# A fused attention and gated-MLP kernel: exponentials behind both shares, wider attention operations, and a band block one slot sooner

## Chip, cores and metric

The kernel runs on one core of a Trainium2 chip. The metric is the device time of one execution in microseconds (us). Every ratio below is the mean time of one kernel's fast runs over the mean of the other's fast runs of the same rounds, so it is not quite the ratio of the medians that stand beside it. A difference counts as faster or slower only beyond 2%.

## The reference

Two branches on the same kind of input, mixed by a gate. Branch A is attention in which each position sees 8 earlier ones, two apart. Branch B is a gated MLP whose second half is normalized and mixed along the sequence.

```python
x = A_x                                             # 1 x 2048 x 1024
g = sigmoid((x * gate_w).sum(-1, keepdims=True))
# A: 32 heads of 32, window W = 8, dilation 2
q, k, v = split(x @ wqkv)
logits = einsum('bhsd,bhswd->bhsw', q, gathered(k)) * scale   # masked where idx < 0
a = einsum('bhsw,bhswd->bhsd', softmax(logits), gathered(v)) @ wo
# B: F = 3584, Fh = F // 2
z = gelu(B_x @ w_in);  z1 = z[..., :Fh];  z2 = layernorm(z[..., Fh:])
b = ((z1 * (w_sp @ z2 + b_sp)) @ w_out)
return g * a + (1 - g) * b
```

## The kernel before

The kernel is one long stream of products on the matrix engine (PE). Most are Strassen-like sets ("quads") of 7 products with 4 PSUM banks. The attention is done by the vector engine (DVE) beside them, in 8 groups of heads; a Python scheduler decides at build time, by an estimated clock, which piece of attention work is put next on DVE and where loads and exponentials go. The first part makes q, k, v and the band products; then come the "z2 pairs", pairs of quads for the second half of branch B. The parts that matter here, with their lines:

```python
# band_blocks(g, first, step, n): q-k products of one group, into banks 4..7
st = band_slots[band_at[0] % 3]; band_at[0] += 1
...
nc.tensor.matmul(banks[4 + h][...], qt[...], kt_[...], ...)     # L355
...
nc.scalar.copy(dst, src)                                         # L363: empties all four banks
# ... then stores of st to band_d, issued by SP (the sync engine)

# strassen(...): one quad                                        (cut)
last_seed[0] = nc.scalar.copy(Y[:, n], X[:, n])                  # L421: seed copy
share(vs, V[:, n])                                               # L427: share copy, into vq_slots
nc.scalar.copy(Z[:, n], Y[:, n])                                 # L432
# chain(...): one lean quad                                      (cut)
last_add[0] = nc.vector.tensor_tensor(out, a, vs, ALU.add)       # L474: the plus
last_seed[0] = nc.scalar.copy(Y[:, n], X[:, n])                  # L487
share(vs, V[:, n])                                               # L493

def mark(bs, N=512, lo=0):                                       # L559: two products that open a new stretch
    for b in bs: nc.tensor.matmul(b[:, lo:N], ...)

def exponential(g): nc.scalar.activation(L[:], L[:], ACT.Exp, ...)   # L631

# maxima(): first operation on a group's logits, waits for their load
tt(att_m[:], L4[:, :, 0:4, :], L4[:, :, 4:8, :], ALU.max)        # L640, then L641 to L643
# products(): attention weights times v, and the sum over the window
for ws in SPLIT[g > FINE]:
    ... tt(p5[:, ws], in0[:, ws], in1[:, ws], ALU.mult)          # L677, 128x2048
for n, ws in enumerate([slice(0, 4)] if g <= FINE else [slice(0, 2), slice(2, 4)]):
    ... tt(a, a, b, ALU.add)                                     # L681, 128x2048

BAND_AT = (1, 3, 6)
def among_bands(g, quad):                                        # groups 2 and 4
    for n in range(7):
        next(quad); step()
        if n + 1 in BAND_AT: band_set(g, x); ...

def quad_step():                                                 # in each z2 pair
    hold[0] = count[0] != 1        # exponentials may go out at this step only
    ...
```

A seed copy starts one bank with the sum that stands in another; PE then goes on adding into it. A share copy takes a sum out of PSUM; in the lean quads a plus on DVE then adds it to what stands in a bank. The last of the three band slots overlaps the memory that the share copy L427 writes into, so the first L427 after the bands of group 2 waits until the store of a band block has left it.

## Time and profile before

| | before |
|---|---|
| time, median of 3 runs | 650.38 us (650.0 to 650.91) |
| span of the profiled run | 649.2 us |
| PE busy | 638.1 us, 98% |
| DVE busy, ACT busy | 519.3 us, 297.8 us |
| waits of PE that the change can reach | 4, of 0.15 to 0.35 us (85.17, 88.03, 189.56, 192.89 us) |

PE's records say when a matmul starts. A wait shows as a gap, and what ended it stands in brackets. Since PE carries everything, I read the result below by the time between two products that all versions share, instead of by the total, in which the start-up alone scatters by over 1 us:

- S1, from the gate product (L996, 44.50 us before, behind all start-up) to the first band products of group 3 (116.15): it holds the band blocks of group 2. Before: 71.65 us.
- S2, from the mark that opens the first z2 pair (183.45; called T below) to the last mark but one (264.06). Before: 80.61 us.

### The profile page before, as it was taken

Reading aid. Unit: us, or ns where it says so; the run is one execution under the profiler, and the core shown is the slowest. Engines: PE = TensorE matmul, PEld = TensorE weight load, DVE = VectorE, ACT = ScalarE, POOL = GpSimd, SP = SyncE. Lnnn points to the kernel's source line nnn. Section 1 sums busy time; section 2 is a strip of 40 time slices with the busy share of each in tenths; the row PEclk is TensorE's granted clock in tenths of the full one; section 3 lists DMA queues with packets and bytes.
Section 4 is the critical chain, followed back from the end, with each engine's and each line's share of the span. In section 5 each row is a group of like instructions: output and inputs, shape, how many; then the busy total and the mean of one; then the engine's idle time right before and its main releaser. Section 6 shows DMA issues by size and latency. Waiting matters only on the chain.

```text
span 649.2 us, 11298 instructions
## 1 busy us (share of the span) xinstructions
PE 638.1 (98%) x4346; PEld 336.4 (52%) x4391; DVE 519.3 (80%) x816; ACT 297.8 (46%) x644; POOL 15.4 (2%) x27
## 2 busy tenths in 40 slices
PE   8999999999999999999999999999999999999997
PEld 4544467444445555444444444444444444868684
DVE  0357988999899999999988766987569999596952
ACT  3547677676776877799643121121121121212110
POOL 2210000000000000001000000000000000000000
PEclk9999999999999999999999999999999999999999
DMA  9979564798688012258994578469587383665401
GB/s 207 198 179 269 126 152 103 175 230 200 122 214 204 1 42 85 66 148 230 258 269 133 130 163 172 120 195 280 100 189 172 86 157 99 111 138 128 124 27 49
DMA packets 227174, 98.19 MB, mean 151 GB/s; under 512 B 174496, under 2 KB 214064, under 8 KB 227120
## 3 DMA queue, kind: packets, MB, share of 16 engines
q1 hardware_dynamic: 226256, 95.70, 61.2%
q0 software_dynamic: 576, 1.57, 0.9%
q8 instruction: 34, 0.56, 0.3%
q10 hardware_dynamic: 288, 0.20, 0.1%
q14 instruction: 20, 0.16, 0.1%
HBM read 44.31 MB, written 36.61 MB: 125 GB/s over the span
## 4 chain that ended last, share of the span: by engine, by line
PE 84%; ACT 4%; DVE 4%; DMA 4%; SPq 2%; issue 2%; ACTq 0%; DVEq 0%
PE psum_all L403 69%; PE psum_all L1487 8%; PE psum_all L293 4%; PE psum_all L303 2%; DMA band_d<-arena 2%; ACT arena L839 2%; PE psum_all L355 1%; DVE arena L677 1%; ACT arena L1178 1%; SPq L189 1%; DVE arena L681 1%; SPq L178 1%; DMA arena<-in_A_wqkv_dram 1%; SPq L194 1%; DVE psum_all L474 1%
## 5 line engine op out<-in xcount | busy, mean ns | idle before, releaser
L403 PE MATMUL psum_all<-arena 128*128 128x512 f16 (+6 forms) x2482 | 503.0, 362 | 3.4 <-issue 0.6
L403 PEld LDWEIGHTS <-arena 128*128 128x128 f16 (+1 forms) x2518 | 245.1, 98 | 253.8 <-issue 4.0
L677 DVE TENSOR_TENSOR arena<-arena,att_A 128x2048 f16<-128x2048 bf16 x64 | 75.5, 1219 | 0.3
L474 DVE TENSOR_TENSOR psum_all<-psum_all,arena 128x512 f32<-128x512 f32 (+1 forms) x78 | 51.0, 669 | 10.1 <-PE psum_all L403 8.3
L1487 PE MATMUL psum_all<-arena 128*128 128x256 f16 (+1 forms) x468 | 51.6, 273 | 0.0
L1487 PEld LDWEIGHTS <-arena 128*128 128x128 f16 x468 | 45.8, 98 | 5.5
L293 PE MATMUL psum_all<-arena 128*128 128x512 bf16 x183 | 42.0, 379 | 1.4 <-issue 0.8
L421 ACT COPY psum_all<-psum_all 128x512 f32<-128x512 f32 (+1 forms) x24 | 12.5, 521 | 66.8 <-PE psum_all L403 66.2
L784 ACT ACTIVATE arena<-psum_all 128x448 bf16<-128x448 f32 x64 | 34.3, 546 | 19.0 <-PE psum_all L403 9.0
L1178 ACT ACTIVATE arena<-psum_all 128x512 bf16<-128x512 f32 x56 | 31.4, 612 | 19.8 <-PE psum_all L403 9.0
L681 DVE TENSOR_TENSOR arena<-arena 128x2048 f16<-128x2048 f16 x32 | 37.9, 1218 | 0.0
L363 ACT CAST arena<-psum_all 128x1988 f16<-128x1988 f32 (+3 forms) x25 | 34.0, 1360 | 3.6 <-PE psum_all L355 3.4
L839 ACT ACTIVATE arena<-arena 128x896 bf16<-128x896 bf16 x32 | 30.9, 980 | 0.0
L546 DVE TENSOR_TENSOR arena<-arena 128x512 f16<-128x512 bf16 (+5 forms) x60 | 30.1, 534 | 0.3
L445 ACT COPY psum_all<-psum_all 128x512 f32<-128x512 f32 (+1 forms) x24 | 12.4, 519 | 37.2 <-PE psum_all L403 36.6
L293 PEld LDWEIGHTS <-arena 128*128 128x128 bf16 x192 | 18.1, 98 | 21.6 <-DMA arena<-in_A_wqkv_dram 0.7
L870 ACT CAST arena<-psum_all 128x512 bf16<-128x512 f32 x40 | 22.1, 592 | 12.5 <-DVE psum_all L474 9.6
L389 DVE TENSOR_TENSOR arena<-arena 128x2048 f16<-128x2048 bf16 x8 | 9.4, 1222 | 21.8 <-ACT gl_s L306 20.9
L427 ACT COPY arena<-psum_all 128x512 f32<-128x512 f32 (+1 forms) x24 | 12.7, 534 | 26.3 <-PE psum_all L403 22.5
L487 ACT COPY psum_all<-psum_all 128x512 f32<-128x512 f32 (+1 forms) x39 | 21.7, 570 | 6.6 <-PE psum_all L403 6.0
L432 ACT COPY psum_all<-psum_all 128x512 f32<-128x512 f32 (+1 forms) x24 | 12.5, 519 | 25.6 <-PE psum_all L403 23.0
L550 DVE TENSOR_TENSOR arena<-arena 128x1024 f16<-128x1024 f16 (+1 forms) x16 | 11.3, 714 | 15.7 <-PE psum_all L403 15.7
(113 smaller groups left out, 530.6 us busy)
## 6 DMA issues: line engine op xcount, KB each, us to landing
arena<-v_d SPq DMA_DIRECT2D x8, 960.0 KB, 7.1
z_d<-arena SPq DMA_DIRECT2D x14, 512.0 KB, 3.4
arena<-z_d SPq DMA_DIRECT2D x14, 512.0 KB, 4.1
zg_d<-arena SPq DMA_DIRECT2D x56, 128.0 KB, 2.2
arena<-zg_d SPq DMA_DIRECT2D x32, 224.0 KB, 3.2
band_d<-arena SPq DMA_DIRECT2D x28, 248.5 KB, 4.6
arena<-in_A_wqkv_dram SPq DMA_DIRECT2D x16, 256.0 KB, 4.3
o_d<-arena SPq DMA_DIRECT2D x4, 1024.0 KB, 6.3
```

The costliest lines, as they stand in the source:

```text
L293: nc.tensor.matmul(ps[:], w[:, t, kt, :], xT[:, kt, 512 * c:512 * (c + 1)], start=(kt == 0), stop=(kt == KT - 1))
L363: nc.scalar.copy(dst, src)
L403: nc.tensor.matmul(bank[:, 0:N], lhsT, rhs, start=(start and m == 0), stop=(m == n - 1), skip_group_check=True)
L474: last_add[0] = nc.vector.tensor_tensor(out[:, n], a[:, n], vs, ALU.add)
L546: return [lambda a=a: nc.vector.tensor_tensor(*a) for a in args]
L677: lambda ws=ws, in0=in0, in1=in1: tt(p5[:, ws], in0[:, ws], in1[:, ws], ALU.mult)), False
L681: lambda a=p3[:, ws], b=p3[:, ws.start + 4:ws.stop + 4]: tt(a, a, b, ALU.add)), not n
L784: nc.scalar.activation(z2[:, i + 8 * a, ZC * c:ZC * (c + 1)], bank[:, 0:ZC], ACT.Gelu_apprx_tanh, accum_out=s1[:, 4 * n + c:4 * n + c + 1])
L839: return nc.scalar.activation(junk, src, ACT.Square, accum_out=(s2, s2h)[x][:, n:n + 1])
L870: nc.scalar.copy((qT_slots, kT_slots)[t][g % 2][:, :, 256 * (c + 2 * x):256 * (c + 2 * x + 1)], bank[:].rearrange("p (n e) -> p e n", e=2))
L1178: last_gelu[0] = nc.scalar.activation(z1s[:, f, a, :], bank[:], ACT.Gelu_apprx_tanh)
L1487: nc.tensor.matmul(bank[:, h], l, r, start=(start and m == 0), stop=(m == len(ab) - 1), skip_group_check=True)
```

## The change

Its intent: release the last exponentials of the attention only when both share copies of a z2 pair are out, so that the pluses of the pair need not wait for ACT; use operations of twice the width where no plus can be held up by them; and put the last band block of group 2 where its evacuation is over by the time the mark needs the banks. In full:

```diff
-                for ws in SPLIT[g > FINE]:
+                for ws in SPLIT[not wide[0]]:
...
-                for n, ws in enumerate([slice(0, 4)] if g <= FINE else [slice(0, 2), slice(2, 4)]):
+                for n, ws in enumerate([slice(0, 4)] if wide[0] else [slice(0, 2), slice(2, 4)]):
...
+    wide = [False]
     SPLIT, FINE = [[slice(n * x, n * x + n) for x in range(8 // n)] for n in (4, 2)], FINE_TO
...
-            if n + 1 in BAND_AT:
+            if n + 1 in (BAND_AT if g != 2 else (1, 3, 5)):
...
         hold[0] = g == NG - 1
+        wide[0] = g in (5, 6, 7)
...
+    wide[0] = False
     load_later(1, clock["PE"] + 3.0, 2.0)
...
-            hold[0] = count[0] != 1
+            hold[0] = count[0] != 4
```

## The prediction

> **What bounds the kernel now.** I read the page's busy table first, then the waits of the matrix engine (PE), then the timelines around those waits, then the chain of waits.
>
> ```profile
> span 649.2 us, 11298 instructions
> PE 638.1 (98%) x4346; PEld 336.4 (52%) x4391; DVE 519.3 (80%) x816; ACT 297.8 (46%) x644; POOL 15.4 (2%) x27
> ```
>
> PE is busy 638.1 of 649.2 us at full granted clock, and the change leaves every matmul in place. Removing work from the Vector engine (DVE, 519.3 us) or the Scalar engine (ACT, 297.8 us) therefore saves nothing by itself: only time in which PE stands still can come back. Of the 11.1 us in which PE is idle, some 2.5 us lie before the kernel is under way (gaps before 12 us) and 3.5 us after the last matmul (645.67 us), and neither is touched. The list of what PE waited for names the rest (us in total, times, longest):
>
> ```profile
> PE psum_all L355 <- ACT arena L363: 0.6, 1, 0.6
> PE psum_all L559 <- ACT arena L363: 0.3, 1, 0.3
> PE psum_all L403 <- ACT psum_all L487: 0.3, 1, 0.3
> PE psum_all L403 <- DVE psum_all L474: 0.3, 1, 0.3
> PE psum_all L403 <- ACT psum_all L421: 0.3, 1, 0.3
> ```
>
> Five waits, 0.3 to 0.6 us each. The timeline of PE puts them at 85.17 (L559), 88.03 (L421), 178.77 (L355), 189.56 (L474) and 259.94 us (L487). Two shorter ones, 0.15 us before 192.89 and 0.12 us before 292.09, show only in finer windows. The "0.16 issue" gaps after band blocks are not waits: 11 matmuls are recorded where the code has 12, so a record is missing there.
>
> Two places belong to the change. The first is group 2:
>
> ```profile
> 79.66 2.54 PE L403 MATMUL psum_all<-arena 128*128 128x512 bf16 x11 [0.16 <-issue]
> 82.12 0.65 PE L355 MATMUL psum_all<-arena 32*64 32x71 bf16 x56
> 82.70 2.12 PE L403 MATMUL psum_all<-arena 128*128 128x512 f16 x12
> 85.17 0.43 PE L559 MATMUL psum_all<-arena 128*128 128x320 bf16 x2 [0.35 <-ACT arena L363]
> 85.44 2.34 PE L403 MATMUL psum_all<-arena 128*128 128x320 bf16 x16
> 88.03 1.25 PE L403 MATMUL psum_all<-arena 128*128 128x320 f16 x8 [0.25 <-ACT psum_all L421]
> ...
> 79.61 1.82 ACT L363 CAST arena<-psum_all 128x1988 f16<-128x1988 f32 x1 [0.74 <-PE psum_all L355]
> 81.32 0.63 ACT L631 ACTIVATE att_L<-att_L 128x512 f16<-128x512 f16 x1
> 81.85 1.55 ACT L870 CAST arena<-psum_all 128x512 bf16<-128x512 f32 x3
> 83.28 1.85 ACT L363 CAST arena<-psum_all 128x1988 f16<-128x1988 f32 x1
> ...
> 87.23 0.43 ACT L427 COPY arena<-psum_all 128x320 f32<-128x320 f32 x1 [1.29 <-DMA band_d<-arena]
> 87.55 0.43 ACT L421 COPY psum_all<-psum_all 128x320 f32<-128x320 f32 x1
> ```
>
> The bands (L355) fill four PSUM banks; ACT empties them in one copy of 1.82 us (L363); the marking matmul L559 needs two of those banks. At 88.03 us PE waits for a seed copy (L421) that stands behind a share copy (L427), and that copy waits for a transfer of bands to leave the memory it writes into.
>
> The second is the first z2 pair:
>
> ```profile
> 184.01 4.62 DVE L677 TENSOR_TENSOR arena<-arena,att_A 128x2048 f16<-128x2048 bf16 x4
> 188.67 0.29 DVE L661 TENSOR_TENSOR att_A<-att_L,att_r 128x256 f16<-128x256 f16 x1
> 188.88 1.16 DVE L474 TENSOR_TENSOR psum_all<-psum_all,arena 128x448 f32<-128x448 f32 x2
> 189.94 2.35 DVE L681 TENSOR_TENSOR arena<-arena 128x2048 f16<-128x2048 f16 x2
> 192.21 1.16 DVE L474 TENSOR_TENSOR psum_all<-psum_all,arena 128x448 f32<-128x448 f32 x2
> ...
> 187.21 0.95 ACT L493 COPY arena<-psum_all 128x448 f32<-128x448 f32 x2
> ```
>
> PE waits for DVE's L474. Its inputs, the share copies (L493), are ready at 187.21 + 0.95 = 188.16 us, before L474 begins at 188.88. DVE came to L474 late, straight out of attention work: here DVE sets the time and ACT doesn't.
>
> **What the Trainium skill says.** "VectorE: DVE Perf Modes", section "The TRN2 errata": operations from SBUF pay a fixed latency each, so a large tile pays it once and small ones each time. The trace agrees: four 2048-wide operations take 4.62 us, so (4.62 - 1.22) / 3 = 1.133 us from start to start, while a 4096-wide one (L1147 starts at 434.48, the next at 436.68) takes 2.20. A merge saves 2 x 1.133 - 2.20 = 0.07 us. "ScalarE: Activation LUTs", section "What ACT_TABLE_LOAD costs", gives 1283 ns for a load and 1380 ns of drain after it. The load is 1283 ns here too, but the drain doesn't show: the load of 185.38 us is followed by its exponential at 186.67. "DMA: Bandwidth & Descriptors", section "Why a DMA increments its semaphore by 16 and not by 1": the engines of a transfer finish independently and all are counted. Here, of the store that L427 waits for, 15 of 16 landings are in by 86.15 us and the last comes at 87.13, after a 16 KB packet of the instruction queue had occupied an engine from 84.46 for 0.96 us.
>
> **The change, part by part.** Matmuls recorded 0.30 or 0.35 us long follow each other faster: 16 of 320 columns in 2.34 us give (2.34 - 0.30) / 15 = 0.136 us from start to start; 512 columns give (2.54 - 0.38) / 10 = 0.216. I count in these steps.
>
> *Bands of group 2 a slot sooner.* Four matmuls of 512 columns (0.86 us) now come after the third band block instead of before it. The bands would start at 82.12 - 4 x 0.216 = 81.26, but the evacuation before them holds the banks until 79.61 + 1.82 = 81.43, and PE wakes some 0.04 us later: 81.47, a new wait of 0.21 us. From there 0.58 us to the next matmul (82.12 to 82.70), 8 x 0.216 and 8 x 0.136: PE reaches the marking matmul at 84.86. ACT's order now has two L870 copies instead of three ahead of the evacuation, which starts near 82.8 and ends near 84.65. So L559 starts at 84.86 instead of 85.17, with no wait: 0.31 us won. But the matmul of 88.03 us, reached at 87.61 before and at 87.30 then, waits for L427, and L427 for the store of the *second* band block, whose evacuation (79.61 to 81.43) hasn't moved. If that store lands at 87.13 again, PE resumes at 88.03 again and the 0.31 us are lost. The store's end hung on an instruction fetch, which follows PE's progress; with the third block 0.65 us earlier it may meet the store at another moment. Landing at 86.15 would remove the wait and yield up to 0.73 us (88.03 to 87.30). I put this part at 0.15 us.
>
> *Wide operations.* The order of the built program has nine merges: six of L677 and three of L681. Worth 9 x 0.07 = 0.6 us of DVE, most of it lost: DVE stands 2.9 us at 169.40 us waiting for a band load, so savings before it vanish. Behind it lie four merges (one L677, one L681, the two that replace the four of 184.01): 0.28 us. L474 moves from 188.88 to 188.60, PE's start from 189.56 to 189.28. PE is ready at 189.12 (the last step before it began at 188.94, plus 0.189 for 448 columns), so a wait of about 0.15 us stays. The wait at 192.89 sits behind the same DVE sequence (L681 twice, unmerged) and moves along: 0.28 us in all, 0.25 with a little doubt.
>
> *Exponentials behind the shares.* In the first pair 1.28 + 0.63 us leave the place ahead of L493, which ends near 186.8 instead of 188.16. L474 wasn't waiting for it: zero. The first gelus shift from 189.47 to about 190.0, into the 2.24 us that ACT then idles before 192.87. The last exponential moves from the fourth pair to the third; its two table loads and 0.63 us fit between the shares (208.8) and the gelus that end at 216.4. Zero for PE.
>
> Sum: 0.15 + 0.25 + 0 = 0.40 us; 650.38 - 0.40 = about 650.0 us. The waits at 178.77, 259.94 and 292.09 us remain.
>
> **Rivals.** (1) *A DMA gate takes the gain of the bands*: the wait at 85.17 goes and the one at 88.03 grows by as much. The unmoved second evacuation speaks for it, the chance position of the fetch against it. Then 650.1. (2) *The share copies were the bound of the first pair*, as the change's description suggests: then both waits there vanish, 0.43 + 0.15 us, and with the bands' 0.31 the time is 649.4. The 0.7 us between the end of L493 and the start of L474 speak against it. (3) *Coarser DVE pieces delay PE*: a 2.2 us operation could stand before an L474 that is needed at once. Against it: wide pieces run only where plain tiles do, which need no L474; the last two end before L474 as the four did. If it happened, +0.3 us. (4) *The exponential of the third pair pushes gelus into PE's bank waits*: up to +1.3 us, one table load; the slack above says no.
>
> **Range and chances.** All that the change can reach on PE is the 0.51 (85.17 - 84.66), 0.41, 0.43 and 0.3 us at four waits, 1.7 us or 0.26%, far below 2%. Runs of the kernel before spread from 650.0 to 650.91. Predicted 650.0; 8 in 10 within 649.1 to 650.9. Faster by over 2%: 0.01; within 2%: 0.98; slower: 0.01.
>
> **What would show it.** A wait of L355 for L363 of about 0.2 us near 81.5; none at L559; the wait for L421 still there at 88 us, with L427 still waiting for the band store; L474 of the first pair about 0.3 us earlier, still straight behind L661, with a smaller wait of PE there; L493 done long before. I am wrong if L427 no longer waits for DMA (more gain), if PE waits at a place with none before, or if the waits after 200 us change size.

## The result, and the profile after

The changed kernel takes 650.11 us in the median (649.78 to 651.18, 6 runs), the kernel before 650.45 us in the same rounds (650.0 to 651.83, 6 runs). The ratio is 0.9995 with a 95% interval of 0.9982 to 1.0008: the same within 2%, and not told from no change at all.

The page of the changed kernel, its span and its busy table:

```profile
span 649.4 us, 11332 instructions
PE 641.5 (99%) x4391; PEld 336.5 (52%) x4391; DVE 518.5 (80%) x807; ACT 297.9 (46%) x644; POOL 15.4 (2%) x27
```

DVE has the nine instructions less (816 to 807) that nine merges make, and is 0.8 us less busy. PE's rise from 638.1 to 641.5 us comes with 45 more recorded matmuls, which were missing from the records before; it is no extra work. The profiled span is 0.2 us *longer* than before, although the median is shorter. The whole list of what PE waited for tells why:

```profile
PE psum_all L303 <- DMA arena<-in_A_x_dram: 1.5, 2, 1.3
PE psum_all L318 <- DVE arena L313: 1.2, 1, 1.2
PE psum_all L355 <- ACT arena L363: 0.6, 1, 0.6
PE psum_all L303 <- DVE arena L325: 0.3, 1, 0.3
PE psum_all L403 <- ACT psum_all L487: 0.3, 1, 0.3
```

In this one execution the first load of the input came 1.3 us late, at 20.5 us, before anything that was changed. All waits that the prediction named as reachable (L559, L474, L421) have left the list. Two gaps too short for this list are new: 0.15 us before the third L355 of group 2 (82.83 us) and 0.14 us at 87.35 us. The waits after 200 us keep their size (0.28 and 0.12 us before, 0.27 and 0.10 us after). By stretches, against the profile before: +1.35 us until the gate product, -0.40 us in S1, -0.76 us in S2, +0.04 us in the rest, +0.22 us at the last product (all from the start times of the same products in both traces).

S1, timeline of the changed kernel around the moved band block, PE and then ACT (columns: start us, us, engine, line, operation, out<-in, count, and in brackets the idle time before and what ended it). Subtract 1.35 to compare with before:

```profile
82.83 0.64 PE L355 MATMUL psum_all<-arena 32*64 32x71 bf16 x56
83.41 2.99 PE L403 MATMUL psum_all<-arena 128*128 128x512 bf16 x16
86.23 0.43 PE L559 MATMUL psum_all<-arena 128*128 128x320 bf16 x2
...
84.15 1.84 ACT L363 CAST arena<-psum_all 128x1988 f16<-128x1988 f32 x1
85.86 1.11 ACT L871 CAST arena<-psum_all 128x512 bf16<-128x512 f32 x2
86.81 0.49 ACT L421 COPY psum_all<-psum_all 128x320 f32<-128x320 f32 x1
88.16 0.42 ACT L427 COPY arena<-psum_all 128x320 f32<-128x320 f32 x1 [0.87 <-PE psum_all L403]
```

The mark L559 starts without a wait, at 86.23 - 1.35 = 84.88 us, 0.29 us sooner than before. But the seed copy L421 starts at 86.81 - 1.35 = 85.46 us, and before it started at 85.46 us as well. ACT simply had one copy L870 (L871 in the changed file, whose later lines stand one lower) ahead of the evacuation moved behind it: between the first evacuation and the seed it does the same work in another order, without a pause. So PE, early at the mark, stands still for the seed: the product at 87.35 us on this trace's own clock starts 0.43 us behind the one before it, where the step is 0.14 us, and the 0.29 us are gone. What S1 did gain comes next: L427 starts at 88.16 - 1.35 = 86.81 us, against 87.23 before, because the band store that it waits for landed sooner. (The bracket names PE, but the product that L427 reads was over by 87.3 us. The store's last landing is recorded at 88.06 us, just ahead of the copy.) The second seed behind L427 is then in time and the 0.41-us step of before vanishes.

S2, timeline of DVE in the changed kernel, and the last share copy of ACT:

```profile
169.56 0.29 DVE L640 TENSOR_TENSOR att_m<-att_L 128x256 f16<-128x256 f16 x1 [2.23 <-DMA att_L<-band_d]
...
184.03 4.49 DVE L677 TENSOR_TENSOR arena<-arena,att_A 128x4096 f16<-128x4096 bf16 x2
188.56 0.29 DVE L661 TENSOR_TENSOR att_A<-att_L,att_r 128x256 f16<-128x256 f16 x1
188.76 1.16 DVE L474 TENSOR_TENSOR psum_all<-psum_all,arena 128x448 f32<-128x448 f32 x2
...
187.25 0.53 ACT L493 COPY arena<-psum_all 128x448 f32<-128x448 f32 x1 [0.23 <-PE psum_all L403]
```

The same wait before the change, from DVE's timeline:

```profile
169.40 0.29 DVE L640 TENSOR_TENSOR att_m<-att_L 128x256 f16<-128x256 f16 x1 [2.88 <-DMA att_L<-band_d]
```

The reader should measure both from the mark T of their own trace (183.45 before, 184.40 after). L640 starts at T - 14.05 before and T - 14.84 after; the plus L474 at T + 5.42 before and T + 4.36 after. So of 1.06 us, 0.79 came because the load of the bands landed sooner relative to PE, and 0.27 from a shorter path on DVE between the two (19.47 to 19.20 us). Which of the two belongs to the change is what the experiments ask.

**Theory A**: the change earns what the two profiles show, 0.40 + 0.76 us. **Theory B**: it earns 0.27 us through the wide operations when the load is late, and something in S1 through the landing of one store; the rest of S2 is when the load that ends the wait at 169 us happens to arrive. **Theory C**, from the change's own description: the exponentials in front of the shares held the pair up.

### The profile page after: what moved, and what is told of

It is laid out like the page before. It is cut to its first block, busy times and chain, and to the rows that moved or that the text cites. A ratio compares the mean times of both kernels' runs of the same rounds, so it can differ in the third digit from the quotient of the medians.

```text
span 649.4 us, 11332 instructions
## 1 busy us (share of the span) xinstructions
PE 641.5 (99%) x4391; PEld 336.5 (52%) x4391; DVE 518.5 (80%) x807; ACT 297.9 (46%) x644; POOL 15.4 (2%) x27
## 4 chain that ended last, share of the span: by engine, by line
PE 90%; ACT 4%; SPq 2%; DMA 1%; DVE 1%; issue 1%; DVEq 0%; ACTq 0%
PE psum_all L403 72%; PE psum_all L1490 8%; PE psum_all L293 6%; PE psum_all L303 2%; PE psum_all L355 2%; ACT arena L840 1%; SPq L178 1%; DMA arena<-in_A_x_dram 1%; ACT arena L1181 1%; PE psum_all L792 1%; ACT arena L785 1%; ACT arena L363 1%; SPq L162 0%; DVE psum_all L474 0%; ACT psum_all L487 0%
## 5 line engine op out<-in xcount | busy, mean ns | idle before, releaser
L677 DVE TENSOR_TENSOR arena<-arena,att_A 128x2048 f16<-128x2048 bf16 (+1 forms) x58 | 74.9, 1329 | 0.3
L474 DVE TENSOR_TENSOR psum_all<-psum_all,arena 128x512 f32<-128x512 f32 (+1 forms) x78 | 51.1, 670 | 11.3 <-PE psum_all L403 8.5
L293 PE MATMUL psum_all<-arena 128*128 128x512 bf16 x192 | 43.3, 379 | 0.1
L421 ACT COPY psum_all<-psum_all 128x512 f32<-128x512 f32 (+1 forms) x24 | 12.5, 521 | 66.1 <-PE psum_all L403 65.4
L681 DVE TENSOR_TENSOR arena<-arena 128x2048 f16<-128x2048 f16 (+1 forms) x29 | 37.7, 1329 | 0.0
L363 ACT CAST arena<-psum_all 128x1988 f16<-128x1988 f32 (+3 forms) x25 | 34.0, 1359 | 3.2 <-PE psum_all L355 2.9
L871 ACT CAST arena<-psum_all 128x512 bf16<-128x512 f32 x40 | 22.1, 593 | 12.5 <-DVE psum_all L474 9.6
L427 ACT COPY arena<-psum_all 128x512 f32<-128x512 f32 (+1 forms) x24 | 12.7, 533 | 26.5 <-PE psum_all L403 23.4
L303 PE MATMUL psum_all<-arena 128*128 128x385 bf16 x128 | 22.7, 330 | 1.8 <-DMA arena<-in_A_x_dram 1.5
```

Of the source, the lines that this page charges most:

```text
L293: nc.tensor.matmul(ps[:], w[:, t, kt, :], xT[:, kt, 512 * c:512 * (c + 1)], start=(kt == 0), stop=(kt == KT - 1))
L303: nc.tensor.matmul(ps[:, 0:VP + 1], xT[:, kt, i * P:(i + 1) * P], wvp[:, kt, :], start=(kt == 0), stop=(kt == KT - 1))
L474: last_add[0] = nc.vector.tensor_tensor(out[:, n], a[:, n], vs, ALU.add)
L677: lambda ws=ws, in0=in0, in1=in1: tt(p5[:, ws], in0[:, ws], in1[:, ws], ALU.mult)), False
L681: lambda a=p3[:, ws], b=p3[:, ws.start + 4:ws.stop + 4]: tt(a, a, b, ALU.add)), not n
```

## The experiments

Twelve runs followed, two of them (e1, e5) of unedited kernels, all correct, all "same" against the kernel before of their own rounds. Their times scatter more than the differences at stake (the kernel before took 650.3 to 655.1 us on the chips of the first two calls), so the findings rest on the stretches, one trace for each run. The expectations name their theories by letters of their own, which each of them explains; only the text between them uses A, B and C as above. This table has the readings of all traces. The times of the S1 group count from the gate product, those of the S2 group from the mark T; all are start times in the trace, in us.

| run | instruction packet: start, length | seed L421 | share L427 released | S1 | L640 | L640 to plus | plus L474 | S2 |
|---|---|---|---|---|---|---|---|---|
| before | 39.97, 0.96 | 40.96 | 42.65 | 71.65 | -14.05 | 19.47 | 5.42 | 80.61 |
| after | 38.20, 1.41 | 40.96 | 42.24 | 71.25 | -14.84 | 19.20 | 4.36 | 79.85 |
| e1 before again | 39.93, 0.93 | 40.96 | 42.62 | 71.62 | -12.92 | 19.47 | 6.55 | 81.72 |
| e2 bands only | 38.07, 1.60 | 40.96 | 42.30 | 71.30 | -12.96 | 19.46 | 6.50 | 81.68 |
| e3 wide only | 39.97, 0.93 | 40.97 | 42.67 | 71.67 | -13.61 | 19.20 | 5.59 | 80.76 |
| e4 exponentials only | 39.95, 0.93 | 40.96 | 42.65 | 71.65 | -14.39 | 19.46 | 5.07 | 80.25 |
| e5 after again | 38.16, 1.56 | 40.96 | 42.34 | 71.35 | -12.98 | 19.19 | 6.21 | 81.38 |
| e6 no share wait | 39.95, 0.93 | 40.96 | 41.32 | 71.24 | -14.31 | 19.47 | 5.16 | 80.34 |
| e7 bands and wide | 38.21, 1.68 | 40.96 | 42.58 | 71.59 | -14.41 | 19.19 | 4.78 | 79.95 |
| e9 load wait filled | 38.19, 1.33 | 40.97 | 42.11 | 71.25 | -11.81 | 16.80 | 4.99 | 80.17 |
| e10 bands, no share wait | 38.06, 1.63 | 40.97 | 41.32 | 71.25 | -14.16 | 19.21 | 5.05 | 80.23 |
| e11 best | 39.94, 0.93 | 40.96 | 41.32 | 71.25 | -13.66 | 17.33 | 3.67 | 79.86 |
| e12 best again | 38.06, 1.52 | 40.97 | 41.32 | 71.25 | -14.63 | 18.31 | 3.68 | 79.86 |

(e8 has another order of PE and is told apart below. "Instruction packet" is the one 16 KB packet of an instruction queue in this stretch.)

Two rules hold over the whole table to 0.02 us:

- S1 = 71.25 + what the release of L427 exceeds 42.24.
- S2 = 79.855 + what the start of the plus exceeds T + 4.68.

They are read from these traces and belong to these orders of work. e8 falls outside both: its S1 is 71.40 with the share released at 42.26, because PE lost 0.14 us at the mark of the group before and the seed came at 41.11; and with another order on DVE its plus starts at T + 5.01 with S2 at 79.96.

The column L640 can be followed one step further back, on the timeline of SP, which gives its instructions in the same order in every run of the table. The second of the two loads that L640 needs is issued at T - 16.88 before, - 17.31 after, - 15.94 in e1, - 15.51 in e5 and - 14.31 in e9, and in all thirteen traces L640 starts 2.5 to 3.0 us behind that. So most of the scatter of 3.0 us is there before the load is issued: SP issues it late. Why was not tried; SP's wait list names the landings of band stores.

### e1: the kernel before, once more

```diff
 (no edit)
```

> The kernel before, unchanged, to learn which of its waits repeat. Two stretches are measured on the matrix engine, free of the start-up: S1 from the gate's matmul to the first bands of group 3 (71.65 us in the first trace of before, 71.25 in that of the changed kernel) and S2 from the marking matmuls of the first z2 pair to those at the head of the z1 stage (80.61 and 79.85). Theory A (the waits follow from the order of the instructions): S1 71.65 and S2 80.61 again within 0.05. Theory B (they follow from when transfers and instruction fetches happen to meet): S1 or S2 moves by 0.2 us or more with no change of the kernel. Total time 650.0 to 651.9 either way.

Measured 651.74 us (650.05 to 653.39), the kernel before 652.31 us in the same rounds, ratio 0.9982 [0.9960, 1.0004]. S1 is 71.62, as in the first trace. S2 is 81.72, 1.11 us more, with nothing changed. DVE's timeline in this run:

```profile
170.29 0.29 DVE L640 TENSOR_TENSOR att_m<-att_L 128x256 f16<-128x256 f16 x1 [3.34 <-DMA att_L<-band_d]
...
189.75 1.16 DVE L474 TENSOR_TENSOR psum_all<-psum_all,arena 128x448 f32<-128x448 f32 x2
```

And the list of PE's waits from 183 to 195 us of the same run (us in total, times, longest):

```profile
PE psum_all L403 <- DVE psum_all L474: 1.4, 1, 1.4
```

The load of the bands let L640 start at T - 12.92, and 19.47 us later, to the hundredth, comes the plus. PE's wait is 1.4 us instead of 0.3. So the 0.76 us that the pair of profiles showed in S2 lie inside the scatter of one and the same kernel. This is against theory A.

### e2: the bands alone

```diff
-            if n + 1 in BAND_AT:
+            if n + 1 in (BAND_AT if g != 2 else (1, 3, 5)):
```

> Only the third band block of group 2 a slot sooner. Theory A1 (order alone): the wait at the marking matmul goes, the wait for the seed copy goes too, S1 falls by 0.4 as in the changed kernel, S2 stays at 80.61. Theory A2 (what is won at the marking matmul is lost one product later to the first seed copy, which now stands behind two output copies): L421 waits of 0.3 us one product after the mark, S1 falls only if the band store lands sooner, by 0 to 0.4. Theory B: S1 anywhere between 71.2 and 71.7. Total time within 0.4 us of before.

Measured 651.13 us (650.63 to 652.4), ratio 0.9978 [0.9958, 0.9997]. S1 is 71.30, 0.35 us under the kernel before; S2 is 81.68 with the late load of this run. The gain in S1 follows the edit.

### e3: the wide operations alone

```diff
-                for ws in SPLIT[g > FINE]:
+                for ws in SPLIT[not wide[0]]:
 ... and the lines that set wide[0]
```

> Only the wide attention operations. Theory A (the Vector engine sets the first z2 pair): S1 stays 71.65, the first L474 of the pair comes 0.28 us sooner, S2 falls by about 0.3. Rival (the share copies behind the exponential are the bound): S2 stays at 80.61, since the exponential still stands ahead of the share copies. Theory B: S2 moves with the wait of L640 for the band load near 169 us. Total time 0 to 0.4 us below before.

Measured 651.36 us (651.03 to 654.69), ratio 0.9988 [0.9962, 1.0014]. S1 unchanged at 71.67. From L640 to the plus DVE takes 19.20 us instead of 19.47, as in the changed kernel. Four merges lie between, so one is worth 0.27 / 4 = 0.067 us. The fall of S2 by 0.3 us, which theory A of this expectation has, did not come: S2 is 0.15 us longer than in the first profile of before, because the load came 0.44 us later.

### e4: the exponentials alone

```diff
-            hold[0] = count[0] != 1
+            hold[0] = count[0] != 4
```

> Only the exponentials moved behind both share copies. Theory A: L493 ends near 187 instead of 188.2, L474 doesn't move, S1 71.65 and S2 80.61 stay. Rival (share copies are the bound): both waits of the first pair shrink, S2 falls by 0.4 or more. Total time as before within 0.2 us by theory A.

Measured 651.17 us (650.56 to 656.71; the two runs above 656 have a granted clock of 0.997), ratio 1.0000 [0.9965, 1.0035]. The last share copy ends at T + 3.38 instead of T + 4.70, 1.32 us sooner. The path from L640 to the plus is 19.46 us, unchanged, and S2 follows the rule with the plus at 5.07. (It is 80.25 and not the expected 80.61 because the load came 0.34 us sooner than in the first trace of before.) Theory C falls: nothing on the path waited for the shares.

### e5: the changed kernel, once more

```diff
 (the change, no further edit)
```

> The changed kernel once more, unedited, as its own control. Two stretches of the PE are read: S1 from the gate product to the first band products of group 3 (71.65 us before, 71.25 after) and S2 from the mark product at about 183 us to that at about 264 us (80.61 before, 79.85 after). If the bands part is a real gain, S1 is 71.20 to 71.35 again. If S2 is set by when the band load of the first z2 pair lands (it was 81.72 in the second run of the unchanged kernel), S2 may be anywhere between 79.8 and 81.5; if the change itself took the 0.76 us of S2, it is below 80.0 again. The 1.27 us of waiting for the first load at 20 us of the changed kernel's profile should be gone if it was start-up scatter and there again if it belongs to the change. Time within 0.3% of the kernel before under all theories.

Measured 650.25 us (649.8 to 651.5), the kernel before 651.43 us, ratio 0.9979 [0.9945, 1.0013]. The late input load at 20 us is not there. S1 is 71.35; S2 is 81.38, which is 1.53 us more than in the first trace of the same kernel. Theory A is out. From the last mark to the end this run has 378.06 us instead of 377.82; that is not explained.

### e6: the kernel before without the wait of the share copy

```diff
             st = band_slots[band_at[0] % 3]
             band_at[0] += 1
+            band_at[0] += (g, first) == (2, 1)    # group 2 avoids the slot that the shares overlap
```

> The kernel before with one edit: the band blocks of group 2 use two band slots that do not overlap the share copies, so that the share copy ahead of the seed copy no longer waits for the store of the bands. Theory A: the 0.41-us wait before the matmul at 88.0 us came from that store, so it goes and S1 falls from 71.65 to about 71.25, although no band block is moved. Rival: the wait came from the vector engine's own queue, and S1 stays at 71.62 to 71.67. S2 is not touched by the edit and says nothing here (79.8 to 81.8).

Measured 650.48 us (649.95 to 650.91), ratio 0.9979 [0.9946, 1.0012]. S1 is 71.24: all that the moved bands ever won, with no band block moved and the wait at the mark still there. Timelines of PE and ACT; line numbers are one higher from this edit on, so L560 is the mark and L428 the share copy:

```profile
85.14 0.43 PE L560 MATMUL psum_all<-arena 128*128 128x320 bf16 x2 [0.35 <-ACT arena L364]
85.42 3.83 PE L404 MATMUL psum_all<-arena 128*128 128x320 bf16 x27
...
85.79 0.48 ACT L428 COPY arena<-psum_all 128x320 f32<-128x320 f32 x1
```

PE runs 27 matmuls from the mark on without a gap. The wait of 0.35 us at the mark costs nothing, because the seed copy behind it isn't out sooner in any version.

### e7: bands and wide operations, exponentials as before

```diff
 (the change without)
-            hold[0] = count[0] != 1
+            hold[0] = count[0] != 4
```

> The changed kernel without its exponential part. S1 about 71.25 as in the changed kernel. In the first z2 pair the share copies should end about 4.70 us after the mark again (3.38 with the part). Theory A (the exponentials are off the path): the plus operation starts 19.20 us after the operation that waits for the band load, whatever the shares do. Rival (they bound it once the load is early and the operations are wide): where that operation starts more than 14.5 us ahead of the mark, the plus waits for the shares and starts no sooner than 4.7 us after the mark, against 4.36 in the changed kernel; even then the PE's wait for it stays 0 to 0.1, because the PE is ready for it only about 5.7 us after the mark.

Measured 651.4 us (650.41 to 652.16), ratio 0.9997 [0.9958, 1.0037]. The path is 19.19 us and the plus starts at T + 4.78, with the shares ending at T + 4.70. The expectation's own test is not quite met: here the two theories give the same start within a tenth, so this run can't say which came last. It bounds the part, though: S2 is 79.95, 0.1 us over the floor. With the exponentials behind the shares, at most that could have been won. S1 is 71.59, the smallest gain of all runs with moved bands (0.07 us), and goes with the longest instruction packet, 1.68 us.

### e8: a band block first in the last group

```diff
-        return [tiles[0], band[1], tiles[1], band[0], tiles[2], band[2], tiles[3]]
+        return [band[1], tiles[0], tiles[1], band[0], tiles[2], band[2], tiles[3]]
```

> The changed kernel with the order of the last group's first two pieces exchanged, so that a band block stands first in it. It aims at the wait of 0.6 us for the band eviction at about 179 us, behind a table load of the scalar engine. If that wait is the order's, it goes and the time from the first band products of the group before to the mark of the last group falls by 0.3 to 0.6 us. Rival: the table load stands ahead of the same evictions wherever the block is, the wait moves to another product, and nothing is gained; or the vector engine's work, which is put in another order, comes later and the wait for the plus operation grows by up to 1 us. Time within 0.3% under all theories.

Measured 651.46 us (650.8 to 651.72), ratio 0.9993 [0.9960, 1.0026]. The wait of 0.61 us for the band eviction became two, of 0.23 us (for L296) and 0.36 us (for L363), 0.59 us together, and the stretch from group 3's bands to T took 67.41 us instead of 67.30. A new wait for the plus of 0.9 us stands at 294.9 us. The rival was right; by these stretches the version is no better, while the time is not told from the kernel before.

### e9: the wait for the load filled with work

```diff
-            yield lambda g=g: t_bands[g] + 1.5, 0.21, lambda: tt(att_m[:], ...      # L640
+            yield lambda g=g: t_bands[g] + {5: 3.4, 6: 4.0}.get(g, 1.5), 0.21, lambda: tt(att_m[:], ...
```

On top of the change. The scheduler now puts the second half of a product ahead of L640.

> The changed kernel with one more edit that leaves all arithmetic alone: the vector engine does the second half of the product that already has its data (2.28 us) and one 0.3-us operation before it asks for the late band load, instead of standing idle 2.2 to 3.5 us for it, and the next maximum comes one 0.69-us operation later. Theory B (the stretch S2 from the mark at 183 us to the one at 264 us is set by when that load lands, through this wait): the wait shrinks below 1 us, the first plus operation starts no later than 4.3 us after the mark whenever the load lands, the PE does not wait for it, and S2 is 79.8 to 80.0 (79.85 to 81.38 in the two runs of the changed kernel, 80.61 and 81.72 in those of the kernel before). Rival (the wait moves to another load, or the exponential behind the load comes late): another vector wait of 1 us or more appears between 168 and 190 us and S2 stays above 80.2. Time: 0.3 to 1.0 us below the kernel before under theory B, too little to be called faster.

Measured 650.38 us (650.29 to 650.76), the kernel before 651.73 us (650.45 to 656.35), ratio 0.9979 [0.9950, 1.0008]. DVE's timeline:

```profile
165.41 4.50 DVE L677 TENSOR_TENSOR arena<-arena,att_A 128x4096 f16<-128x4096 bf16 x2
169.94 0.29 DVE L661 TENSOR_TENSOR att_A<-att_L,att_r 128x256 f16<-128x256 f16 x1
171.82 0.29 DVE L640 TENSOR_TENSOR att_m<-att_L 128x256 f16<-128x256 f16 x1 [1.59 <-DMA att_L<-band_d]
...
188.62 1.16 DVE L474 TENSOR_TENSOR psum_all<-psum_all,arena 128x448 f32<-128x448 f32 x2
```

The load came later than in any other run, T - 11.81, so the expected "below 1 us" was missed: 1.59 us of waiting stayed, the plus came at 4.99 instead of by 4.3, and S2 is 80.17 instead of 79.8 to 80.0. The edit can hardly have made the load late: ahead of this wait it leaves the order on SP and ACT as it was, and the load was late already when SP issued it. But the path is 16.80 us, 2.4 us shorter. By the rule, and as an estimate, the changed kernel with this load would have had its plus at -11.81 + 19.20 = 7.39 and S2 at 82.57; e9 measured 80.17. This is the knob that theory B asked for: with the path behind the load made shorter, the plus comes sooner than the load would else allow, and S2 follows it.

### e10: the changed kernel without the wait of the share copy

```diff
 (the change, and e6's line)
```

> The changed kernel with the share copy's wait for the band store taken away as in e6. If the bands part and the store wait were two separate costs, S1 would be about 70.95 (71.65 less 0.29 at the mark less 0.41 at the share). If the seed copy behind the two value copies (a PE wait of 0.30 start to start at 87 us in the changed kernel) has taken the place of the first, the two do not add and S1 is 71.20 to 71.30, the same as with either alone.

Measured 650.52 us (649.98 to 652.91), ratio 0.9989 [0.9962, 1.0015]. S1 is 71.25, as with e6's edit alone. The moved band block and the removed wait don't add. S2 is 80.23 with the plus at 5.05, by the rule.

### e11 and e12: two versions meant to beat both

```diff
 e11: the change without its bands part, with e6's line and e9's edit
 e12: the change with e6's line and e9's edit
```

> A version meant to beat both: the kernel before with the wide operations, the exponentials behind both shares, the band slots of e6 in place of the moved bands, and the filled load wait of e9. S1 71.20 to 71.30, S2 79.8 to 80.0, no PE wait for a plus operation in the first z2 pair, so about 1.1 us less than the profile of before and 0.2 to 1.5 us less than the changed kernel, by where its load lands: 648.8 to 650.0 us where the kernel before takes 650.4.

> The changed kernel with the edit of e9 (load wait filled) and the band slots of e6. By the rule read from the runs so far, S2 is 79.86 us plus whatever the first plus operation's start exceeds 4.68 us after the mark, and that start follows the operation that waits for the load by 16.8 to 17.4 us (19.2 without e9's edit). So a load that lets that operation start 12.2 us ahead of the mark or sooner gives 79.85 to 79.95; one as late as in e9 (11.8) gives 80.2. S1 is 71.24 to 71.26 whatever the band store does. From the last mark to the end 377.8 to 378.1, as in every run whose late order was not changed (it was 378.87 in e11; if it is over 378.5 here, the loss at the end belongs to filling the wait). Time about 0.5 to 1.5 us under the kernel before in the same rounds, not told from 2%.

e11 measured 650.61 us (649.38 to 650.9), the kernel before 651.73, ratio 0.9976 [0.9950, 1.0003]. e12 measured 650.05 us (649.75 to 650.58, 6 runs), the kernel before 651.36 (651.03 to 658.47, 11 runs), ratio 0.9967 [0.9933, 1.0001]. Both have S1 at 71.25 and S2 at 79.86, the two floors. In e12 DVE did not wait for the load at all (L678, L641 and L475 are the L677, L640 and L474 of before):

```profile
163.94 4.49 DVE L678 TENSOR_TENSOR arena<-arena,att_A 128x4096 f16<-128x4096 bf16 x2
168.68 0.28 DVE L641 TENSOR_TENSOR att_m<-att_L 128x256 f16<-128x256 f16 x1
...
186.98 1.39 DVE L475 TENSOR_TENSOR psum_all<-psum_all,arena 128x448 f32<-128x448 f32 x2 [1.43 <-PE psum_all L404]
```

Now DVE waits 1.43 us for PE at the plus, where PE waited for DVE before. All six runs of e12 are below all eleven of the kernel before on that chip, but the interval touches 1 and the gain is 0.2 to 0.3%, so it is not called faster. The changed kernel was not timed on that chip, so the two are compared by their stretches only. What stays open is the end: from the last mark on e11 takes 378.87 us, e12 378.30 and the kernel before 377.82. e12's value falls between the two marks set for it, e9 with the same fill has 377.82, and in e11 0.4 us of the loss are a wait of PE for a seed copy at 615.7 us. The filled wait is neither shown nor cleared as the cause.

## Why the prediction came out as it did, point by point

**The sum was right, 0.40 us predicted against 0.34 us between the medians**, but the measurement can't tell 0.34 from 0, and the single terms did not come out as written: the term for the bands was half of what came, by another path, and that for the wide operations reaches PE only with a late load. That the sum came so near is luck.

*What bounds the kernel, and that nothing near 2% could come of it.* Right. Only waits of PE came back, and the four places named were the right ones.

*Bands, 0.15 us.* The new wait of L355 came as written (its start at 82.83 - 1.35 = 81.48 us, 81.47 predicted; as a gap 0.15 us), and so did the free mark with its 0.29 us (0.31 predicted). The step that failed is the next one, that PE would run on to the gate at 88 us. It stops for the seed copy, whose start is 40.96 or 40.97 us in every version of the table, because ACT works without a pause between the evacuation and it. The prediction moved an L870 copy behind the evacuation and did not count it in front of the seed. So the 0.29 us are lost, to ACT's queue and not, as rival 1 had it, to a DMA. The other half of the step, the store that "may meet [the fetch] at another moment", is where the gain comes from, and it is systematic. The DMA view of the kernel before from 84.4 to 85.5 us shows one packet of an instruction queue (columns: packets, MB, share of the 16 engines in that window):

```profile
q8 instruction: 1, 0.02, 5.5%
```

The same view of the changed kernel has it from 84.0 to 85.5 us, which is 82.7 to 84.2 on the clock of before:

```profile
q8 instruction: 1, 0.02, 5.9%
```

Measured from the gate product it starts at 39.93 to 39.97 us in all six traces with the bands unmoved and at 38.06 to 38.21 us in all with the bands moved, e8 included. With it the store lands 0.07 to 0.54 us sooner, roughly the more so the shorter the packet takes (soonest with 1.33 us in e9, latest with 1.68 us in e7). The landings say more. The store goes out in two halves of 16 landings each. In all six traces with the bands unmoved the packet runs during the second half, whose last landing comes 0.9 to 1.2 us behind the other 15. In all eight with the bands moved it runs during the first half: there the last landing comes 1.2 to 1.8 us late, and in the second half only 0.2 to 0.8 us. That the packet itself delays the store fits this but wasn't tried alone; it is argued. A rival that was not tried either is the third block's own store, which the moved block sends out sooner, too. That the store's landing sets S1 is shown, by e6 and e10. The term measured 0.40, 0.35, 0.30, 0.07 and 0.40 us in the five traces that have it without another edit in S1 (after, e2, e5, e7 and e9, against 71.65), 0.30 in the mean: twice the predicted 0.15. The upper end of "up to 0.73 us" was wrong too; the seed stops it at 0.41.

*Wide operations, 0.25 us.* The duration was right: 0.28 predicted for DVE's path, 0.27 measured in e3, e5, e7, e10 and after. With the load of the profile before, all of it would reach PE by the rule for S2. The step from there to PE was sound only for a load that lands late. Where the plus starts by T + 4.68 anyhow, a shorter path saves nothing. In the changed kernel's first trace 0.32 of the 1.06 us by which the plus came sooner were of no use: 5.42 - 4.68 = 0.74 us could be won, and 0.76 were measured.

*Exponentials, 0.* Right: 1.32 us sooner shares, path unchanged (e4). In e7 the shares come within 0.1 us of mattering, so the part is worth at most 0.1 us beside the wide operations. Rivals 3 and 4 did not come: in no run of the table with the wide operations is S2 longer than its rule gives, and in the changed kernel's profile the waits after 200 us kept their size.

*The signs of being wrong.* One came: PE has a gap at a place where it had none, 0.14 us at 87.35 us, for the first seed. This is the lost step above. The wait for L421 at 88 us, which was to stay, is gone. L427 still waited for the store (not by its bracket, but by the landing at 88.06 us).

*What was missing.* The prediction took the landing at 169.40 us as a fixed point "so savings before it vanish". It is the largest scatter behind the start-up: L640 starts from T - 14.84 to T - 11.81, and S2 of unedited kernels ranges over 1.11 us (before, e1) and 1.53 us (after, e5), three and four times the change's sum. Rival 2 seemed to come true in the first pair of profiles, both waits of the pair gone and 0.76 us won. It had not; an earlier load did it. One pair of profiles would have proved the wrong theory.

## What to carry to other kernels

Measure a change between two instructions that both versions have, near it on each side, and profile the unchanged kernel twice before believing a difference of a microsecond: the moment at which a load arrives may scatter more than the change earns. Before counting a freed wait, walk the queue of the engine that ended it to its next user; work moved behind one instruction stands in front of the next. And where an engine stands idle for a transfer, putting work that already has its data in front of that wait can be worth more than speeding the work behind it: 2.4 us of path in e9, against 0.27 us from the wide operations. By the rule for S2, neither of them reaches PE when the load is early.

## What the Trainium skill lacked or had wrong

- "Runtime: NRT & Kernel Launch", section "Instruction fetch mechanics", is the page for the instruction queues. What no page gives is what their packets do to a kernel's own transfers. Every profile here has 34 packets, 0.56 MB, on one instruction queue and some 20 on another; the single 16 KB packet in S1 takes 0.93 to 1.68 us among band stores, and in the half of the store during which it runs one landing of 16 comes 0.9 to 1.8 us behind the others. Its time moves with the order of PE's instructions: 1.8 us sooner for a band block 0.64 us sooner.
- "DMA: Bandwidth & Descriptors", section "Why a DMA increments its semaphore by 16 and not by 1", says that the engines of a transfer finish independently; the traces agree (15 of 16 landings by 86.15 us, the last at 87.13). It gives no measure of how far apart they finish: the last landing of the band store before the seed came 0.2 to 1.2 us behind the other 15 in the fourteen traces.
- "ScalarE: Activation LUTs", section "What ACT_TABLE_LOAD costs": the 1283 ns of the load agree, the 1380 ns of drain do not show where exponential and gelu change places (copy of before ends at 185.36, load at 185.38, exponential at 186.67 us).
